# A two-pass attention kernel with a folded feed-forward layer: written step order and plain PSUM evacuation, against engine orders from a list scheduler, VectorE transposes and evacuation on three engines

## The chip, the cores and the metric

The kernel runs on one core of one Trainium2 chip. All times are device microseconds (us) of that core. A run's time is some 2 us longer than the span that the profile shows, because the span goes from the first to the last recorded instruction. Executions differ by a few tenths of a per cent; those whose clock state made them more than 1.5% slower than the fastest of the same kernel are called slow and are left out of every comparison here.

Engine names: PE is the matmul engine (PEld its weight loads), DVE is VectorE, ACT is ScalarE, POOL is GpSimd, SP is SyncE. In both kernels all loads of `x` are issued by GpSimd and are converted from float32 to fp16 on the way; all stores are issued by SyncE. "The queue" below is short for the 16 DMA engines that carry all transfers. PSUM is the memory into which the matmuls write; to evacuate a result is to copy it from there to SBUF, where the other tiles lie. The granted clock is the share of its full clock that PE was granted, by the profile.

## The reference, cut to what matters

```python
# x: (4, 12480, 128), inducing: (32, 128), w_in: (128, 2048), w_out: (2048, 128)
def mab(q, kv):
    s = (1/sqrt(128)) * (q @ kv.T)
    a = softmax(s)                     # + 1e-9 in the denominator
    return a @ kv
h   = mab(inducing, x)                 # per batch: 32 x 128, needs ALL of the batch's x
y   = mab(x, h)                        # per token: softmax over the 32 rows of h
out = gelu_exact(y @ w_in) @ w_out     # per token
```

The kernel uses that `y` is a mixture of 32 rows of `h` and that the argument of the GELU is small here: it puts the 32 rows of `h` through a quadratic form of the feed-forward layer once per batch (a chain of small steps ending in a 32 x 128 matrix `q`), and each token's output is its 32 softmax weights times `q`. Checks on the device add up whether that was admissible; if not, a general path runs.

What matters for time is the dependence. A batch's whole input (six tiles of 2048 tokens and a short tail) must be in before its `q` exists, and no output of that batch can be stored before that. So 27.7 MB come in, the two weights included (13.8 MB as fp16), and 25.6 MB go out, through the same 16 DMA engines, and output starts a batch later than input.

## The kernel before

One unit is 2048 tokens. The A side of a unit loads it, transposes it, makes scores against `inducing`, takes exp, turns the exponentials and gathers `hun += e1.T @ x`. The B side makes scores against `h`, takes exp, and writes four blocks of 512 columns of `o`, then stores them. The steps that the change touches:

```python
    def a_weights(bt, u):                      # turn the exponentials: PE, then a copy by VectorE
        e1 = bt.live.pop(("e1", u.idx))
        e1t_ps = ps.tile([128, 8, 128], FP16, tag="big", bufs=4)
        for ci in range(u.nci):
            nc.tensor.transpose(e1t_ps[: u.p, ci, : u.rows],
                e1[: u.rows, ci * u.p : (ci + 1) * u.p], identity_h[: u.rows, : u.rows])
        e1t = sb.tile([128, 4, 128], FP16, tag="e1t", bufs=2)
        nc.vector.tensor_copy(out=e1t[...], in_=e1t_ps[...])
    ...
    def b_out(bt, u, ci, on_act):              # one of four blocks of o
        at = ps.tile([128, 4, 128], FP32, tag="big", bufs=4)
        nc.tensor.matmul(at[...], e2[...], bt.q[...], start=True, stop=True)
        if on_act:   # four ScalarE quarters, each with its own scale
            ...
        else:
            nc.vector.tensor_tensor(out=ov[: u.p, ci, :, :], in0=at[...], in1=rr2[...], op=ALU.mult)
        if ci == u.nci - 1:
            nc.sync.dma_start(out=out[...], in_=o[...])
    ...
    LAG = n_u + 5                              # the B side runs 12 steps behind the A side
    def at_step(s):
        ...                                    # a0, a1, a2: units s, s-1, s-2; b0, b1: units s-12, s-13
        if a0: load_next(); a_transpose(bat(a0), a0, 0)
        if a1: a_score(bat(a1), a1)
        pump()                                 # one stage of the chain of a finished batch
        if b1: b_sum(...); b_out(..., 0, False); b_out(..., 1, lone)
        ...
    for _ in range(3): load_next()             # five tiles, then the weights, then three more tiles
    nc.gpsimd.dma_start(out=w_in_h, in_=moe_w_in)
    nc.gpsimd.dma_start(out=w_out_h, in_=...)
    for _ in range(3): load_next()
    for s in range(n_all + LAG + 1): at_step(s)
```

The framework's own scheduler may reorder what is written, within each engine, before it is compiled.

Of the kernel before, what the change touches and what calls it, by code (L numbers as in the profile page):

```python
# [8 lines left out]
FP32 = mybir.dt.float32  # L9
# [15 lines left out]

EPS = 2.0**-10
# [10 lines left out]
TP = TAIL // 2  # L37


class Unit:  # L40


    def __init__(self, b, idx):
        self.b = b
        self.idx = idx
        self.tail = idx == NFULL
        self.t0 = idx * SGT
        self.p = TP if self.tail else 128
        self.nj = 1 if self.tail else 4
        self.nci = 2 if self.tail else 4  # L50
        self.nc = self.nj * self.nci
        self.cols = self.nci * self.p
        self.rows = 32 * self.nj


@with_exitstack
def kernel(
# [22 lines left out]
    def a_load(u):  # L80
        xh = sb.tile([128, 16, 128], FP16, tag="xh", bufs=9)
        src = x[u.b, u.t0 : u.t0 + u.nc * u.p, :].rearrange("(p c) d -> p c d", p=u.p)
        nc.gpsimd.dma_start(out=xh[: u.p, : u.nc, :], in_=src)  # L83
        x_tiles[(u.b, u.idx)] = xh

    a_load(units[0][0])
# [9 lines left out]
    indT_ps = ps.tile([C, M], FP32, tag="misc")  # L96
# [30 lines left out]
    class Batch:  # L127
        def __init__(self, b):
            self.b = b
            self.rr2 = pre.tile([128, n_u, 4, 4], FP32, tag="rr2")  # L130
            nc.gpsimd.memset(self.rr2[:, NFULL, :, :], 1.0 / M)
            self.xT = xt_pool.tile([128, N], FP16, tag="xT", name=f"xT{b}")
            self.r1 = pre.tile([128, NFULL + 1], FP32, tag="r1")
            nc.gpsimd.memset(self.r1, 0.0)
# [6 lines left out]
    def a_transpose(bt, u, half):  # L141
        xh = x_tiles[(u.b, u.idx)]
        c0, c1 = (0, min(8, u.nc)) if half == 0 else (8, u.nc)
        if c1 <= c0:
            return
        tr = ps.tile([128, 8, 128], FP16, tag="big", bufs=4)
        for c in range(c0, c1):
            nc.tensor.transpose(  # L148
                tr[:, c - c0, : u.p], xh[: u.p, c, :], identity_h[: u.p, : u.p]
            )  # L150
        dst = bt.xT_of(u, c0, c1).rearrange("q (c p) -> q c p", p=u.p)
        if half == 0:
            nc.vector.tensor_copy(out=dst, in_=tr[:, : c1 - c0, : u.p])  # L153
        else:
            nc.scalar.activation(out=dst, in_=tr[:, : c1 - c0, : u.p], func=AF.Copy)  # L155

    def a_score(bt, u):
        s1 = ps.tile([128, 512], FP32, tag="sc", bufs=2)
        for j in range(u.nj):
            nc.tensor.matmul(  # L160
                s1[32 * j : 32 * j + 32, : u.cols],
                indT,
                bt.xT_of(u, j * u.nci, (j + 1) * u.nci),
# [3 lines left out]
        e1 = sb.tile([128, 512], FP16, tag="e1", bufs=2)  # L167
        nc.scalar.activation(
            out=e1[: u.rows, : u.cols],
            in_=s1[: u.rows, : u.cols],  # L170
            func=AF.Exp,
            scale=SCALE,
            accum_out=bt.r1[: u.rows, u.idx : u.idx + 1],
# [3 lines left out]
    def a_weights(bt, u):  # L177
        e1 = bt.live.pop(("e1", u.idx))
        e1t_ps = ps.tile([128, 8, 128], FP16, tag="big", bufs=4)
        for ci in range(u.nci):  # L180
            nc.tensor.transpose(  # L181
                e1t_ps[: u.p, ci, : u.rows],
                e1[: u.rows, ci * u.p : (ci + 1) * u.p],
                identity_h[: u.rows, : u.rows],
            )
        e1t = sb.tile([128, 4, 128], FP16, tag="e1t", bufs=2)
        nc.vector.tensor_copy(  # L187
            out=e1t[: u.p, : u.nci, : u.rows], in_=e1t_ps[: u.p, : u.nci, : u.rows]
        )
        bt.live[("e1t", u.idx)] = e1t  # L190

    def a_gather(bt, u):
        e1t = bt.live.pop(("e1t", u.idx))
        xh = x_tiles.pop((u.b, u.idx))
        for ci in range(u.nci):
            for j in range(u.nj):
                nc.tensor.matmul(  # L197
                    bt.hun[32 * j : 32 * j + 32, :],
                    e1t[: u.p, ci, 32 * j : 32 * j + 32],
                    xh[: u.p, j * u.nci + ci, :],  # L200
                    start=(u.idx == 0 and ci == 0),
                    stop=(u.tail or (u.idx == NFULL - 1 and j > 0)) and ci == u.nci - 1,
                )
# [15 lines left out]
    def check_gelu(bt, pt, hs):  # L219


        b = bt.b
        zsq = pre.tile([128, NBLK, M], FP32, tag="zsq")
        nc.scalar.activation(out=zsq, in_=pt, func=AF.Square)
        ssq = pre.tile([128, NBLK], FP32, tag="ssq")
        nc.vector.tensor_reduce(out=ssq, in_=zsq, axis=AX.X, op=ALU.add)
        left = pre.tile([128, NBLK], FP32, tag="left")
        nc.vector.scalar_tensor_tensor(
            out=left, in0=hs, scalar=-1.0 / M, in1=hs, op0=ALU.mult, op1=ALU.mult
        )  # L230
        nc.vector.tensor_tensor(out=left, in0=left, in1=ssq, op=ALU.add)
        quart = pre.tile([128, NBLK], FP32, tag="quart")
        nc.vector.scalar_tensor_tensor(
            out=quart, in0=ssq, scalar=1.0 / 6.0, in1=ssq, op0=ALU.mult, op1=ALU.mult
        )
        nc.vector.tensor_tensor(out=left, in0=left, in1=quart, op=ALU.add)
        sums = pre.tile([128, 2], FP32, tag="sums")
        nc.vector.scalar_tensor_tensor(
            out=quart,
            in0=left,  # L240
            scalar=(2.0 * CGELU / EPS) ** 2 * M,
            in1=left,
            op0=ALU.mult,
            op1=ALU.mult,
            accum_out=sums[:, 0:1],
        )
        nc.vector.tensor_reduce(out=sums[:, 1:2], in_=ssq, axis=AX.X, op=ALU.add)
        tot_ps = ps.tile([128, 2], FP32, tag="misc")
        nc.tensor.matmul(tot_ps, ones_f, sums, start=True, stop=True)
        right = pre.tile([128, 2], FP32, tag="right")  # L250
        nc.vector.tensor_copy(out=right, in_=tot_ps)
        nc.vector.tensor_tensor(
            out=checks[:, b, 4:5], in0=right[:, 0:1], in1=right[:, 1:2], op=ALU.is_le
        )
        nc.vector.tensor_scalar(
            out=checks[:, b, 5:6],
            in0=right[:, 1:2],
            scalar1=Z_LOW * DFF * M,
            scalar2=None,
            op0=ALU.is_ge,  # L260
        )

    def precompute(bt):
        hun_sb = pre.tile([128, C], FP32, tag="hun_sb")
        nc.scalar.activation(out=hun_sb, in_=bt.hun, func=AF.Copy)
        r1c = pre.tile([128, 1], FP32, tag="r1c")
        nc.vector.tensor_reduce(out=r1c, in_=bt.r1, axis=AX.X, op=ALU.add)
        r1s = pre.tile([128, M], FP32, tag="r1s")
        nc.vector.tensor_scalar(
            out=r1s, in0=stack4, scalar1=r1c, scalar2=None, op0=ALU.mult  # L270
        )
        yield
        h_ps = ps.tile([128, 2, M], FP32, tag="misc")
        nc.tensor.matmul(h_ps[:, 0, :], ones_f, r1s, start=True, stop=True)
        nc.tensor.matmul(h_ps[:, 1, :], hun_sb, stack4, start=True, stop=True)
        yield
        rr1 = pre.tile([128, M], FP32, tag="rr1")
        nc.vector.reciprocal(out=rr1, in_=h_ps[:, 0, :])
        in_range(rr1, 1.0 / R_HIGH, 1.0 / R1_LOW, bt.b, 0)
        bt.hT = pre.tile([128, M], FP16, tag="hT")  # L280
        nc.vector.tensor_tensor(out=bt.hT, in0=h_ps[:, 1, :], in1=rr1, op=ALU.mult)

        yield
        pt_ps = ps.tile([128, NBLK, M], FP32, tag="misc")
        for blk in range(NBLK):
            nc.tensor.matmul(
                pt_ps[:, blk, :],
                w_in_h[:, blk * 128 : (blk + 1) * 128],
                bt.hT,
# [3 lines left out]
        yield  # L293
        pt = pre.tile([128, NBLK, M], FP32, tag="pt")
        nc.scalar.activation(out=pt, in_=pt_ps, func=AF.Copy)
        hs = pre.tile([128, NBLK], FP32, tag="hs")
        nc.vector.tensor_reduce(out=hs, in_=pt, axis=AX.X, op=ALU.add)
        slope = pre.tile([128, NBLK], FP32, tag="slope")
        nc.vector.tensor_scalar(
            out=slope,  # L300
            in0=hs,
            scalar1=2.0 * CGELU / M,
            scalar2=0.5,
            op0=ALU.mult,
            op1=ALU.add,
        )
        offs = pre.tile([128, NBLK], FP32, tag="offs")
        nc.vector.scalar_tensor_tensor(
            out=offs,
            in0=hs,  # L310
            scalar=CGELU / (M * M),
            in1=hs,
            op0=ALU.mult,
            op1=ALU.mult,
        )
        sl = pre.tile([128, NBLK, M], FP32, tag="sl")
        nc.vector.tensor_tensor(
            out=sl,
            in0=pt,
            in1=slope.unsqueeze(2).broadcast_to([128, NBLK, M]),  # L320
            op=ALU.mult,
        )
        gl = pre.tile([128, NBLK, M], FP16, tag="gl")
        nc.vector.tensor_tensor(
            out=gl,
            in0=sl,
# [66 lines left out]
    def b_out(bt, u, ci, on_act):  # L393
        if ci >= u.nci:
            return
# [310 lines left out]
```

## Time and profile before

| kernel before | |
|---|---|
| time, median of 3 | 160.44 us (160.09 to 160.69) |
| span of the profiled run | 158.4 us, mean granted clock 0.923 |
| busy: PE, DVE, ACT, POOL | 122.8, 106.0, 77.2, 17.9 us |
| DMA queues' packet time | 45.7% + 39.8% + 0.7% of the span: 136.5 us |
| first and last store issued | 49.8 and 147.3 us |
| transfers of the last store all but over | 152.3 us (last packet ends at 152.6) |

Here are lines of the profile page of the kernel before. In the lines of digits, each digit is one of 40 slices of the span (3.96 us each) and gives the busy share in tenths; DMA is the mean of the 16 DMA engines, and GB/s is what they moved in each slice. The last line is from the table of DMA issues: the count, the size of each, and the median time from issue to landing.

```profile
span 158.4 us, 3683 instructions
...
DVE  2122321547967997977988988788869979799100
...
DMA  2999999999999999999999766243469865899930
GB/s 43 207 211 214 197 202 218 213 213 211 214 212 213 301 305 321 313 318 316 267 312 354 304 267 265 103 166 132 161 286 408 366 269 211 346 387 408 430 137 14
...
out_dram<-o SPq DMA_DIRECT2D x24, 1024.0 KB, 4.4
```

The DMA digits are 9 from the second slice to slice 22, that is to about 87 us. There the loads end: the last is issued at 79.4 us and lands 7.2 us later, at 86.6. The digits then fall to 7, 6, 6, 2, 4, 3, 4, 6: the queue has little to do, although about 18 of the 25.6 MB of output still have to leave. In the median a store lands 4.4 us after its issue, of which the transfer alone takes 2.4; so most stores of this kernel do not queue, they are waited for.

The next lines are the view of busy time in chosen windows, for the kernel before. Columns: start and end, length; busy us and number of instructions of PE, PEld, DVE, ACT and POOL; then the granted clock, the DMA share (it adds up the times of packets, and reads somewhat above 1 where the queue is full) and GB/s.

```profile
core 0: us, PE busy (x) PEld busy (x) DVE busy (x) ACT busy (x) POOL busy (x), PEclk, DMA share, GB/s
3.00:92.00 89.00, 77.50 (x1026) 47.36 (x1027) 58.16 (x157) 44.74 (x87) 15.88 (x36) 0.98 1.06 255
92.00:152.30 60.30, 45.28 (x437) 20.56 (x434) 47.43 (x141) 31.13 (x83) 0.11 (x1) 0.88 0.69 280
```

Up to 92 us the transfers hardly pause (only from 88 us on does the share fall, to 0.68). After 92 us there are 60.3 us at share 0.69, which is 41.6 us of transfer and 18.7 us of idle queue, while VectorE still has 47.4 us of work and PE 45.3 us. The largest single term of the time that could be saved stands here.

### The profile page before, as it was taken

The page shows a single profiled execution, that of the slowest core. Times are in us where ns is not written, and L with a number is a line of the kernel's source. Part 1 is how long each engine was busy: PE and PEld are TensorE (multiplying, and loading weights), DVE is VectorE, ACT ScalarE, POOL GpSimd, SP SyncE. Part 2 cuts the span into 40 slices and gives each one's busy share as a digit, 9 for nine tenths or more (in the row PEclk, how much of TensorE's full clock was granted, in tenths as well). Part 3 has the DMA queues.
Part 4 walks back from the last instruction along what each step waited for, and adds up shares of the span by engine and source line. Part 5 has one row for each costly group of instructions (what it writes and reads, how often), then busy time and mean ns, then how long its engine had stood idle before and what let it go on. Part 6 is the DMA issues. An engine that isn't in the chain of part 4 may idle for free. (4 is left out here: it accounts for less than half of the span.)

```text
span 158.4 us, 3683 instructions
## 1 busy us (share of the span) xinstructions
PE 122.8 (78%) x1459; PEld 67.9 (43%) x1459; DVE 106.0 (67%) x303; ACT 77.2 (49%) x171; POOL 17.9 (11%) x44
## 2 busy tenths in 40 slices
PE   0388957899999999988899999878998578984000
PEld 0356634676655555454444645435344233321000
DVE  2122321547967997977988988788869979799100
ACT  3035642578574555734445548344476824885000
POOL 7811120222111201110110000000000000000000
PEclk9999996999999999999999999999999955699655
DMA  2999999999999999999999766243469865899930
GB/s 43 207 211 214 197 202 218 213 213 211 214 212 213 301 305 321 313 318 316 267 312 354 304 267 265 103 166 132 161 286 408 366 269 211 346 387 408 430 137 14
DMA packets 10091, 39.73 MB, mean 251 GB/s; under 512 B 2992, under 2 KB 3792, under 8 KB 6992
## 3 DMA queue, kind: packets, MB, share of 16 engines
q0 software_dynamic: 6112, 13.83, 45.7%
q1 hardware_dynamic: 3952, 25.58, 39.8%
q8 instruction: 13, 0.21, 0.5%
q14 instruction: 14, 0.11, 0.2%
HBM read 27.67 MB, written 25.56 MB: 336 GB/s over the span
## 5 line engine op out<-in xcount | busy, mean ns | idle before, releaser
L148 PE MATMUL tr<-identity_h,xh 128*128 128x128 f16 x392 | 35.2, 237 | 7.3 <-DMA xh<-in_x_dram 6.2
L148 PEld LDWEIGHTS <-xh 128*128 128x128 f16 x392 | 26.2, 107 | 16.5 <-issue 7.7
L83 POOL DMA_DIRECT2D xh<-in_x_dram x28 | 15.1, 538 | 59.6 <-PE hun_888 L197 17.2
L187 DVE COPY e1t<-e1t_ps 128x512 f16<-128x512 f16 (+1 forms) x28 | 10.8, 387 | 11.9 <-PE e1t_ps L181 11.5
L417 DVE TENSOR_TENSOR o<-at,rr_426 128x512 f32<-128x512 f32 (+1 forms) x26 | 16.1, 652 | 1.0 <-PE at L401 0.8
L417 DVE TENSOR_TENSOR o<-at,rr_118 128x512 f32<-128x512 f32 (+1 forms) x26 | 16.1, 652 | 0.9 <-PE at L401 0.7
L417 DVE TENSOR_TENSOR o<-at,rr_883 128x512 f32<-128x512 f32 (+1 forms) x20 | 12.8, 658 | 0.2
L153 DVE COPY xT_120<-tr 128x1024 f16<-128x1024 f16 (+1 forms) x7 | 4.4, 630 | 10.8 <-PE tr L148 10.8
L417 DVE TENSOR_TENSOR o<-at,rr_1484 128x512 f32<-128x512 f32 (+1 forms) x19 | 11.4, 659 | 0.1
L155 ACT ACTIVATE xT_120<-tr 128x1024 f16<-128x1024 f16 x6 | 6.1, 1021 | 10.4 <-PE tr L148 10.4
L197 PEld LDWEIGHTS <-e1t 128*32 128x32 f16 x392 | 8.1, 97 | 5.8 <-issue 3.2
L360 PEld LDWEIGHTS <-hT 128*32 128x32 f16 x100 | 4.4, 94 | 10.3 <-issue 9.8
L160 PEld LDWEIGHTS <-indT 128*32 128x32 f16 x100 | 4.9, 94 | 8.9 <-issue 6.8
L155 ACT ACTIVATE xT_1486<-tr 128x1024 f16<-128x1024 f16 x6 | 6.1, 1022 | 4.9 <-PE tr L148 4.7
L410 ACT ACTIVATE o<-at,rr_1484 128x128 f32<-128x128 f32 (+1 forms) x25 | 7.2, 369 | 2.3 <-PE at L401 1.6
L155 ACT ACTIVATE xT_885<-tr 128x1024 f16<-128x1024 f16 x6 | 6.1, 1022 | 4.4 <-PE tr L148 4.2
L410 ACT ACTIVATE o<-at,rr_883 128x128 f32<-128x128 f32 (+1 forms) x21 | 6.1, 373 | 2.9 <-DVE rr_883 L387 2.8
L155 ACT ACTIVATE xT_428<-tr 128x1024 f16<-128x1024 f16 x6 | 6.1, 1019 | 1.4 <-PE tr L148 1.3
L153 DVE COPY xT_428<-tr 128x1024 f16<-128x1024 f16 (+1 forms) x7 | 4.4, 627 | 2.0 <-PE tr L148 1.9
L348 DVE TENSOR_TENSOR q<-q_ps,strand 128x512 f16<-128x512 f32 x4 | 2.8, 692 | 3.8 <-PE q_ps L346 3.8
L153 DVE COPY xT_1486<-tr 128x1024 f16<-128x1024 f16 (+1 forms) x7 | 4.3, 621 | 0.8 <-PE tr L148 0.8
L153 DVE COPY xT_885<-tr 128x1024 f16<-128x1024 f16 (+1 forms) x7 | 4.3, 620 | 0.6 <-PE tr L148 0.6
(434 smaller groups left out, 231.1 us busy)
## 6 DMA issues: line engine op xcount, KB each, us to landing
out_dram<-o SPq DMA_DIRECT2D x24, 1024.0 KB, 4.4
xh<-in_x_dram POOLq DMA_DIRECT2D x24, 512.0 KB, 11.5
w_in_h<-in_moe_w_in_dram POOLq DMA_DIRECT2D x1, 512.0 KB, 14.4
w_out_h<-in_moe_w_out_dram POOLq DMA_DIRECT2D x1, 512.0 KB, 17.3
out_dram<-o SPq DMA_DIRECT2D x4, 96.0 KB, 4.9
xh<-in_x_dram POOLq DMA_DIRECT2D x4, 48.0 KB, 10.8
ind_s<-in_inducing_dram SPq DMA_DIRECT2D x1, 16.0 KB, 1.8
```

The lines of the kernel that those rows point to most:

```text
L83: nc.gpsimd.dma_start(out=xh[: u.p, : u.nc, :], in_=src)
L148: nc.tensor.transpose(tr[:, c - c0, : u.p], xh[: u.p, c, :], identity_h[: u.p, : u.p])
L153: nc.vector.tensor_copy(out=dst, in_=tr[:, : c1 - c0, : u.p])
L155: nc.scalar.activation(out=dst, in_=tr[:, : c1 - c0, : u.p], func=AF.Copy)
L160: nc.tensor.matmul(s1[32 * j : 32 * j + 32, : u.cols], indT, bt.xT_of(u, j * u.nci, (j + 1) * u.nci), start=True, stop=True,)
L187: nc.vector.tensor_copy(out=e1t[: u.p, : u.nci, : u.rows], in_=e1t_ps[: u.p, : u.nci, : u.rows])
L197: nc.tensor.matmul(bt.hun[32 * j : 32 * j + 32, :], e1t[: u.p, ci, 32 * j : 32 * j + 32], xh[: u.p, j * u.nci + ci, :], start=(u.idx == 0 ...
L348: nc.vector.tensor_tensor(out=bt.q, in0=q_ps.unsqueeze(1).broadcast_to([128, 4, 128]), in1=strand.unsqueeze(2).broadcast_to([128, 4, 128]) ...
L360: nc.tensor.matmul(s2[32 * j : 32 * j + 32, : u.cols], bt.hT, bt.xT_of(u, j * u.nci, (j + 1) * u.nci), start=True, stop=True,)
L410: nc.scalar.activation(out=ov[: u.p, ci, j, :], in_=at[: u.p, j, :], func=AF.Copy, scale=rr2[: u.p, ci, j : j + 1],)
L417: nc.vector.tensor_tensor(out=ov[: u.p, ci, :, :], in0=at[: u.p, : u.nj, :], in1=rr2[: u.p, ci, : u.nj].unsqueeze(2).broadcast_to([u.p, u. ...
```

## The change

The intent: make every engine's instruction order from a plan rather than by hand; start output as soon as the first batch allows; and spread the work that VectorE does over ScalarE and GpSimd, so that transfers never wait. The diff, cut to its core:

```diff
+class Plan:                       # a list scheduler: pieces with cost per engine, dependencies, buffers
+    def run(self):
+        ...                       # repeatedly takes the piece that could start first; ties within 0.12 us
+                                  # go by key, and a batch's chain (key -1) may win by up to 0.4 us
+        self.pieces.sort(key=lambda p: p.at)
+        for p in self.pieces: p.emit(p.engine)
+def pin_order(tc):                # ties each instruction to the one before it on its engine, so
+    ...                           # that the framework's scheduler can't reorder them

-    xh ... bufs=9                 +    xh ... bufs=XBUFS        # 11
-    for _ in range(3): load_next()          # weights behind five tiles
+    for k, u in enumerate(order):
+        add_load(u)
+        if k == NFULL: add_weights()        # weights behind all seven tiles of batch 0
+    for i in range(FILLERS): ...            # 8 matmuls on zeros before the first tile arrives

-            nc.tensor.transpose(e1t_ps[...], e1[...], identity_h[...])
-        nc.vector.tensor_copy(out=e1t[...], in_=e1t_ps[...])
+        # a_score now puts tokens on partitions in blocks of 32; e1 is held as fp16 pairs
+        nc.vector.transpose(out=pairs(e1t)[: u.p, :n], in_=pairs(e1)[: u.p, :n])   # 32x32 blocks, as int32

-    b_out: block 1 on ScalarE in the last steps only, all others on VectorE
+    AWAY = (0,)                   # block 0: plain copy by ScalarE, then scaled in place by GpSimd
+    other blocks: VectorE (0.61 us) or four ScalarE quarters (1.0 us), as the plan decides
-    LAG = n_u + 5
+    key (k + BEHIND, n)           # B side of unit k ranks with A side of unit k + 13, where both could start
```

Smaller parts: three PSUM buffers for scores and small results instead of two and one, three buffers `e2` instead of two, the square of the check on VectorE instead of ScalarE, and the general path's loop over batches rolled into a loop on the device.

## The prediction

> **What bounds the kernel before** (busy time in chosen windows). (a) 3 to 50 us: only loads move, 207 to 214 GB/s, DMA share above 1; first store issued at 49.8 us. (b) 50 to 92 us: DMA share 1.00 at 307 GB/s, PE 92%, DVE 85% busy. (c) 92 to 147 us: loads are over, DMA at 0.44, 0.58, 0.78; DVE is 81 to 89% busy and ends the chain of waits. Then 4.6 us until the last store lands (152) and 6.4 us of closing (span 158.4).
>
> DMA work: 24.4 loads of 0.52 MB at 212 GB/s, 2.47 us each, 60 us; two weights 5 us; 24.4 stores of 1.05 MB at 430 GB/s, 2.44 us each, 59.5 us: 125 us. From 3 to 152 us that leaves 24 us of idle DMA, nearly all in (c): stores begin too late, then compute cannot feed them.
>
> **What the change does.**
> - Weights behind batch 0's tiles: batch 0 complete about 5 us earlier (the transposes waited 3 us for a tile at 22 to 25 us). PE fillers spare some half-clock transposes (eight: 1.03 against 0.62 us), worth little while DMA-bound.
> - The chain goes first and output follows at once, instead of a fixed lag of 12 steps: first store at about 34 us (batch 0 landed 21, gathered 24, chain 8, first tile 2) instead of 49.8.
> - VectorE, counted in the instruction order: evacuations with scaling 85 to 52 (0.60 us start to start), xT copies 24 to 30, PSUM copies of e1t (0.34 us) replaced by transposes of 256 words, which I estimate at 0.34 us too (the pace of the measured copies; Trainium skill, "VectorE: DVE Perf Modes", the three transpose paths: 311 ns for a 128x128 in bf16; no trace yet). About 101 to 87 us.
> - ScalarE: 44 to 80 scaled quarters (0.26 us), 24 plain copies (0.51), 6 fewer xT copies (0.92): about 69 to 84 us.
> - GpSimd: 24 multiplications of 128x512. Skill, "GPSIMD Engine Reference", 4497 ns for 2048 columns: my estimate 1.1 to 1.3 us each, 29 us, beside 15 us of DMA issue; off the critical path, for a block of o has 2.4 us.
> - PE: 104 transposes gone (0.32 us per unit); pieces stay whole, where single score matmuls between `at` matmuls cost 0.32 us each, as much as four together. About 115 to 95-100 us.
>
> **Sum.** DMA (125 us) then exceeds every engine: DVE 87, ACT 84, PE about 98. If it never idled: 3 + 125 + 1 + 6.4 gives a span of 136, time 138 us. I allow 5 us of idle DMA, as the pinned order follows a model whose errors turn into waits, and PE at 80% in the mixed stage is close. Prediction 143 us, 11% faster; range 138.5 to 149. Faster 0.95, same 0.04, slower 0.01.
>
> **What would show it.** First store issued at 31 to 37 us; DMA at 300 or more GB/s from there to the end, no stretch of 4 us under 0.5; DVE busy 85 to 95 us; transposes 0.35 to 0.45 us each; GpSimd multiplications 1.1 to 1.4 us; last compute at about 131.
>
> **What would make it wrong.** GpSimd stuck in order: a load waiting for a free buffer holds back a multiplication, hence a store, or the reverse. Multiplications far slower beside VectorE. The granted clock at half in the store-only end (0.63 at 130 to 140), which makes `at` 0.60 instead of 0.38 us. Loads and stores together slower than apart. Strided weights (e1t in pairs) or score inputs slowing PE.

## More of the kernel before

The stores, from the timeline of SyncE in the kernel before (start, length up to the last, then the group):

```profile
49.79 97.89 SPq L425 DMA_DIRECT2D out_dram<-o  x28
```

The first of 28 stores is issued at 49.79 us, and the group ends 97.89 us later.

## The result, and the profile after

Ratios are the mean time of one kernel's fast runs over the mean of the other's in the same rounds, with a 95% interval, so they are not quite the ratio of the medians that are quoted.

| | before | after |
|---|---|---|
| time, median (rounds of this comparison) | 160.56 us | 141.1 us (140.5 to 141.8) |
| ratio | | 0.8796 (0.8751 to 0.8841) |
| span, clock of the profiled run | 158.4, 0.923 | 138.7, 0.918 |
| busy PE, DVE | 122.8, 106.0 | 101.6, 96.4 |
| busy ACT, POOL | 77.2, 17.9 | 88.5, 42.6 |
| DMA packet time (share times span) | 136.5 us | 98.6%: 136.8 us |
| first store issued, transfers of the last all but over | 49.8, 152.3 | 43.2, 134.2 (last packet ends at 134.7) |

The change is 12.0% faster. The packet time is the same: the same transfers are packed into 20 us less. The same lines of the page, for the kernel after (a slice is 3.47 us):

```profile
span 138.7 us, 3625 instructions
...
DVE  1354334264999997996989998756999879888000
...
DMA  3999999999999999999999999999889799999960
GB/s 30 197 213 214 215 208 188 216 214 211 214 213 211 267 314 318 307 336 340 325 315 277 295 314 312 318 345 413 369 361 378 309 418 380 390 425 418 416 236 7
...
out_dram<-o SPq DMA_DIRECT2D x24, 1024.0 KB, 8.3
```

The DMA digits are 9 almost throughout; the lowest before the end is a 7. The time from issue to landing of a store has gone from 4.4 to 8.3 us: stores now stand in a queue. The windows of the kernel after, with the columns as before:

```profile
3.00:92.00 89.00, 72.99 (x1126) 44.95 (x1126) 65.96 (x187) 61.33 (x145) 28.29 (x41) 0.96 1.07 262
92.00:134.20 42.20, 28.57 (x245) 12.14 (x245) 30.16 (x97) 27.16 (x81) 12.47 (x12) 0.87 0.95 384
```

Compare with the two rows of before. Up to 92 us both kernels keep the queue full, and both have moved nearly the same: 89 us at 255 GB/s are 22.7 MB, at 262 GB/s 23.3 MB. So the earlier start of the stores has gained 0.6 MB by then, some 1.5 us at the rate of the end, and of that the kernel before lost 1.3 us by idling from 88 us on. What the earlier stores carried, the loads gave up: the last load of the kernel after lands at 97.6 us instead of 86.6. The difference is in what the engines had got done under the same transfers: VectorE 66.0 against 58.2 us, ScalarE 61.3 against 44.7, GpSimd 28.3 against 15.9. After 92 us the kernel after has 42.2 us at share 0.95: 40.1 us of transfer, 2.1 idle. Of the 19.7 us by which the span shrank, 16.6 are idle queue time taken away after 92 us (18.7 less 2.1), 1.5 are less transfer left at 92 us (41.6 less 40.1), and 1.6 are a shorter closing behind these windows (6.1 and 4.5 us to the end of the span).

The stores in the timeline of SyncE, kernel after:

```profile
43.19 85.96 SPq L648 DMA_DIRECT2D out_dram<-o  x28
```

The first is at 43.19 us, where the prediction had 31 to 37; the last is issued at about 128.

The chain of waits that ended last, first by engine and then by line, in the kernel after:

```profile
DVE 12%; DMA 10%; PE 9%; ACT 7%; issue 2%; POOL 1%; DVEq 0%; ACTq 0%; SPq 0%
DMA out_dram<-o 10%; DVE o L638 6%; PE at L601 4%; ACT o L631 3%; PE s L558 2%; ACT e L570 2%; ACT o L263 1%; DVE xT L261 1%; DVE left L502 1%; POOL o L623 1%; DVE zsq L490 1%; ACT e L298 1%; PE q_ps L450 1%; DVE hit L333 0%; ACT pt L388 0%
```

`DMA out_dram<-o` is now its first entry: blocks of `o` wait until an earlier store has left its buffer. In the kernel before, no DMA appears in that part of the page (shown here in the same form); the chain could be followed only for the last 3 us, and is VectorE writing `o`:

```profile
DVE 2%; PE 0%; issue 0%
DVE o L417 1%; DVE hit L209 0%; PE tot_ps L518 0%; DVE tot L526 0%; DVE failed L528 0%; DVE rr_1484 L387 0%
```

### The profile page after: what moved, and what is told of

It reads as the page before. It is cut to its first block, busy times and chain, and to the rows that moved or that the text cites. A ratio compares the mean times of both kernels' runs of the same rounds, so it can differ in the third digit from the quotient of the medians.

```text
span 138.7 us, 3625 instructions
## 1 busy us (share of the span) xinstructions
PE 101.6 (73%) x1371; PEld 57.1 (41%) x1371; DVE 96.4 (69%) x284; ACT 88.5 (64%) x226; POOL 42.6 (31%) x60
## 5 line engine op out<-in xcount | busy, mean ns | idle before, releaser
L601 PE MATMUL at<-q,e 128*128 128x512 f16 (+1 forms) x104 | 35.6, 387 | 5.9 <-ACT o L631 1.4
L623 POOL TENSOR_TENSOR o<-o,rr 128x512 f32<-128x512 f32 x24 | 25.0, 1042 | 43.5 <-ACT o L263 35.2
L638 DVE TENSOR_TENSOR o<-at,rr 128x512 f32<-128x512 f32 (+1 forms) x55 | 34.6, 659 | 5.3 <-DMA out_dram<-o 2.4
L272 PE MATMUL tr<-identity_h,xh 128*128 128x128 f16 x392 | 28.3, 223 | 5.3 <-DVE o L638 2.4
L261 DVE COPY xT<-tr 128x1024 f16<-128x1024 f16 (+1 forms) x32 | 20.4, 649 | 12.3 <-PE tr L272 12.1
L631 ACT ACTIVATE o<-at,rr 128x128 f32<-128x128 f32 (+1 forms) x85 | 24.2, 370 | 3.4 <-DMA out_dram<-o 2.5
L298 ACT ACTIVATE e<-s 128x512 f16<-128x512 f32 (+1 forms) x28 | 15.3, 546 | 11.5 <-PE s L286 10.9
L263 ACT ACTIVATE xT<-tr 128x1024 f16<-128x1024 f16 (+1 forms) x20 | 19.1, 960 | 5.2 <-PE tr L272 5.2
L263 ACT ACTIVATE o<-at 128x512 f32<-128x512 f32 x24 | 14.5, 603 | 5.5 <-DMA out_dram<-o 3.4
L570 ACT ACTIVATE e<-s 128x512 f16<-128x512 f32 (+1 forms) x28 | 14.8, 559 | 3.9 <-PE s L558 3.9
L320 PE MATMUL hun<-xh,e1t 128*32 128x128 f16 x392 | 11.0, 230 | 6.1 <-DVE e1t L312 6.1
L601 PEld LDWEIGHTS <-e 128*128 128x128 f16 (+1 forms) x104 | 9.1, 102 | 12.6 <-issue 8.0
L582 PEld LDWEIGHTS <-e 128*128 128x128 f16 (+1 forms) x104 | 5.6, 99 | 5.7 <-ACT e L570 2.4
## 6 DMA issues: line engine op xcount, KB each, us to landing
xh<-in_x_dram POOLq DMA_DIRECT2D x24, 512.0 KB, 18.7
w_out_h<-in_moe_w_out_dram POOLq DMA_DIRECT2D x1, 512.0 KB, 18.7
```

Source lines behind the costliest of these rows:

```text
L261: nc.vector.tensor_copy(out=out, in_=in_)
L263: nc.scalar.activation(out=out, in_=in_, func=AF.Copy)
L272: nc.tensor.transpose(tr[:, c - c0, : u.p], xh[: u.p, c, :], identity_h[: u.p, : u.p])
L298: nc.scalar.activation(out=e1[: u.p, : u.nc // 2, :, :], in_=s1[: u.p, : u.nc, :].rearrange("r (a b) i -> r a i b", b=2), func=AF.Exp, sca ...
L320: nc.tensor.matmul(bt.hun[32 * j : 32 * j + 32, :], e1t[: u.p, c // 2, :, c % 2], xh[: u.p, c, :], start=u.idx == 0 and c < 4, stop=c + 4 ...
L570: nc.scalar.activation(out=e2[: u.rows, : u.cols], in_=s2[: u.rows, : u.cols], func=AF.Exp, scale=SCALE,)
```

## The experiments

The theory after the result: the kernel after is set by the DMA queue, and the gain is the idle queue time after 92 us, filled because the planned order brings more of the engines' work in front of 92 us. The rivals: (1) the gain comes from less work on the engines, that is from VectorE's transposes and from the blocks given to ScalarE and GpSimd; (2) it comes from the first batch being complete earlier; (3) GpSimd, which issues loads and scales blocks in one order, now holds something back. The twelve runs were made in three groups, each on one chip beside its own runs of the kernel before (medians 160.94, 160.69 and 160.09).

### Halving the stores, in both kernels

To see what binds each kernel, half of the bytes of each store were left out, with all the computing kept. The results are wrong (half of the output is never written).

```diff
-  out=out[base : base + u.nc * u.p, :].rearrange("(p c) d -> p c d", p=u.p),
-  in_=o[: u.p, : u.nc, :],
+  out=out[base : base + u.nc * u.p, :].rearrange("(p c) d -> p c d", p=u.p)[:, : u.nc // 2, :],
+  in_=o[: u.p, : u.nc // 2, :],
```

For the kernel after:

> The changed kernel, but each store moves only half of its columns (wrong result on purpose); the order of instructions is the same. Theory D (the changed kernel waits on the DMA queues from 3 us to 134 us): 24.4 stores cost 1.2 us less each, 30 us of DMA work go, and the time falls to where compute binds, 115 to 128 us. Rival C (the pinned order and the engines set the pace, the queues are merely kept full by it): within 2% of 141, 138 or more.

For the kernel before:

> The kernel before with stores of half the columns (wrong on purpose). Theory D says of it that only 50 to 92 us was bound by DMA and that VectorE and PE set the rest, so little is won: 150 to 160 us. Rival R (the kernel before was bound by DMA all along, as its 125 us of transfers suggest, and the change only shortens the ends): 130 to 142.

Measured: the kernel after fell to 130.6 us (0.8167 of before, 0.8092 to 0.8242; span 128.7). The kernel before only fell to 157.45 us (0.9816, 0.9736 to 0.9897; span 154.6), though the same 30 us of packet time or so were taken from it. The fall of the kernel after is clear, but it stops 2.6 us above the range that the theory had given (115 to 128): the engines bind earlier than expected. The windows of the halved kernels, the kernel after first, from 75 us to its last store:

```profile
75.00:123.00 48.00, 39.43 (x461) 19.37 (x457) 43.34 (x125) 39.55 (x114) 16.62 (x16) 1.00 0.56 208
```

The halved kernel before, from 75 us to its last store:

```profile
75.00:149.00 74.00, 60.98 (x644) 29.96 (x643) 62.60 (x181) 39.83 (x100) 1.27 (x4) 0.93 0.42 149
```

In the halved kernel after, VectorE is busy 43.3 of 48 us, and the queue has a share of 0.56. So the queue does bind the kernel after, but the next limit, the engines, lies only 10 us below: a saving of transfers beyond that would give nothing more. In the kernel before, halving the stores leaves the queue at 0.42 and the time nearly unchanged: that kernel was bound by its engines in their order, and a saving of transfers would have helped it little.

### The order alone

The kernel after with everything but the order put back: transposes of `e1` on PE with VectorE's copy, no blocks for GpSimd, no fillers, nine tiles, weights behind five tiles. The plan (made anew for these pieces), the pinning and the small changes to buffers stay.

```diff
-XBUFS = 11            +XBUFS = 9
-AWAY = (0,)           +AWAY = ()
-FILLERS = 8           +FILLERS = 0
-        if k == NFULL: add_weights()
+        if k == 4: add_weights()
-  a_turn: nc.vector.transpose(...)       # and the score layout that goes with it
+  a_flip: nc.tensor.transpose(...) x4;  a_turn: nc.vector.tensor_copy(...)
```

> The changed kernel with its parts undone and only the planned, pinned order and the merged pieces kept: e1t by PE and PSUM copy, no ScalarE copy plus GpSimd multiplication, weights after five tiles, no fillers, 9 buffers of x; planned anew. Theory O (the order alone keeps the queues full, and the parts only make slack behind them): 141 to 146. Rival P (each part is covered by the slack of the others, together they carry the gain): 149 or more.

Measured: 144.69 us, 0.9025 (0.8943 to 0.9106): 9.7 of the 12 per cent. Its windows:

```profile
3.00:92.00 89.00, 74.50 (x1098) 50.38 (x1098) 64.30 (x184) 50.50 (x139) 15.41 (x29) 0.92 1.07 262
92.00:138.50 46.50, 33.74 (x369) 16.05 (x361) 40.32 (x117) 33.25 (x103) 0.00 (x0) 0.97 0.86 349
```

Up to 92 us it moves just as much as the kernel after, at 262 GB/s. Then 46.5 us at 0.86, against 60.3 at 0.69 in the kernel before. VectorE has been given no relief at all here (104.9 us in total against 106.0), and yet it had 64.3 us of it behind it at 92 us instead of 58.2, and fewer pauses afterwards (40.3 busy of 46.5 us). Its stores start only 1.4 us earlier than in the kernel before (49.79), so an earlier first store is not what the order gains by:

```profile
48.40 86.39 SPq L657 DMA_DIRECT2D out_dram<-o  x28
```

This run leaves two things open. The general path rolled into a loop is still in it: from the last packet of a store to the end of the span it takes 3.5 us, the kernel before 5.8, so some 2.3 of the 15.7 us by which its span is shorter are probably not the order's. And the plan also chooses the engine of many copies and blocks (ScalarE is busy 83.8 us here, 77.2 before); that choice, the cheaper matmuls described next and the order of the pieces as such were not taken apart.

The order also makes the same matmuls cheaper. Both kernels run 1459 of them, at nearly the same clock (0.923 and 0.928), and PE was busy 122.8 us before and 108.2 here. By line: the 392 gather matmuls took 16.1 us before and 11.1 here, the score matmuls of the B side 14.9 and 9.3. Four 32-column matmuls written next to each other run together in parts of the array; the framework's order had put others between them (a gather of 16 came out as 1, 13 and 2). The Trainium skill, "TensorE: Matmul & The Clock Gate", Part 3 (packing small matmuls), describes multiple matmuls running concurrently in one array when each has its own tile of it. The two totals agree with that.

### The order without the pin

```diff
-    pin_order(tc)
```

> The changed kernel, all parts kept, but the planned order is not pinned, so the framework's own scheduler may reorder, and the instruction lists do differ on every engine. Theory O: matmul groups are split again and output blocks fall behind, idle DMA returns after 95 us: 146 to 156. Rival P: the work saved is what counts, and the half-store run shows 10 us of slack: under 144.

Measured: 149.76 us, 0.9321 (0.9247 to 0.9394). The windows of this run:

```profile
3.00:92.00 89.00, 71.41 (x979) 43.84 (x979) 52.59 (x152) 51.50 (x124) 25.99 (x39) 0.83 1.06 256
92.00:145.00 53.00, 41.76 (x393) 18.30 (x392) 39.23 (x118) 35.68 (x103) 14.66 (x15) 0.81 0.77 314
```

Here the framework may still reorder what the plan wrote, and about 5 points of the 12 are lost (0.9321 against 0.8796, in two groups of runs). Up to 92 us it has done only 52.6 us of VectorE work; after that the queue has 0.77. The profiled run had a lower clock (0.817), but that isn't the main cause: another run of it with a clock of 0.885 took 149.39 us, where the kernel after with the same clock took 141.98 us (in another group). Of its gain over the kernel before, some 4 us are closing (1.8 us from the last packet to the end of the span, 5.8 before). The converse, the kernel before with its written order pinned, does not build: the framework reports a deadlock, so it could not be tried. What pinning alone does to the written order stays open.

### The loading side: weights behind the first batch, fillers, eleven tiles

The order alone, with these three put in again:

```diff
 # against the order alone
-XBUFS = 9             +XBUFS = 11
-FILLERS = 0           +FILLERS = 8
-        if k == 4: add_weights()
+        if k == NFULL: add_weights()
```

> Planned and pinned order, weights behind batch 0, fillers and 11 buffers of x, but e1t by PE and no ScalarE copy plus GpSimd multiplication. Theory L (of the 3.6 us that the parts add to the order, most comes from the loading side): 141 to 143. Rival S (the savings of VectorE and PE matter only when both are gone, each alone was covered by the other): 143.5 to 145, like the order alone.

Measured, in five rounds: 141.26 us, 0.8832 (0.8799 to 0.8865). With the kernel after in the same group:

> The changed kernel once more, as the control on this chip for the three runs beside it: 0.88 of before, about 141 us. Both theories alike.

That measured 140.28 us, 0.8784 (0.8733 to 0.8835). The intervals overlap. So the order and the loading side give all but about half a point; what VectorE's transposes and the two extra engines add is under what these rounds resolve. Between the order alone and this kernel lie 1.9 points, though across two groups of runs; the three parts of the loading side were not taken apart.

Late weights alone, in the kernel before:

```diff
-    for _ in range(3): load_next()     +    for _ in range(5): load_next()
     ... weights ...
-    for _ in range(3): load_next()     +    for _ in range(1): load_next()
```

> The kernel before, with the two weights loaded behind batch 0's tiles and nothing else. Both theories: the PE's 3 us wait at 22 to 25 us goes, and the engines, which bind from there on, shift by about that: 157 to 159. If the start does not reach the end (the stages after it have slack): 160 to 161.

Measured: 159.65 us, 0.9948 (0.9867 to 1.0028): no difference that these runs resolve, and a median between the two ranges that were expected. A first batch that is complete earlier brought nothing measurable to this kernel, whose B side starts at a fixed step. Rival (2) falls as a cause by itself; within the planned order it has at most a share of the 1.9 points of the loading side.

### The VectorE transposes: taken out of the kernel after, put into the kernel before

```diff
 # a_peturn, against the kernel after
-  a_turn: nc.vector.transpose(...)
+  a_flip: nc.tensor.transpose(...) x4;  a_turn: nc.vector.tensor_copy(...)
```

> The changed kernel with the weights e1t turned by PE and copied out of PSUM as before, planned anew. Theory D: PE gets 24 x 0.32 us back, VectorE about the same; PE was 84 to 91% busy in 50 to 90 us, and PSUM buffers are shared, 0 to 4 us slower, 141 to 145. Rival V (the VectorE transposes are the gain): 148 or more.

Measured: 141.23 us, 0.8803 (0.8738 to 0.8868), against 0.8796 for the kernel after: no difference.

```diff
 # b_turn: the kernel before, with a_score, a_exp, a_turn, a_gather of the kernel after
-            a_weights(bat(a1), a1)
+            a_turn(bat(a1), a1)
```

> The kernel before with only the VectorE transposes of e1t (and the score layout they need). PE loses 24 x 0.32 us, VectorE stays. Theory O: the order around it still splits groups and leaves the output late: 155 to 160. Rival P (PE work is what binds the kernel before): all of 8 us, 151 to 154.

Measured: 165.51 us, 1.0278 (1.0178 to 1.0379). Both expectations missed: it is slower, with 96 fewer matmuls. Since the interval reaches under 1.02, it isn't certain that the loss exceeds two per cent. Three views of the trace of this run say where a part of it comes from. First, the timeline of GpSimd, whose sequencer issues the loads; in brackets is the idle time before and what ended it:

```profile
11.68 0.53 POOL L83 DMA_DIRECT2D xh<-in_x_dram  x1 [1.88 <-DMA xh<-in_x_dram]
...
31.70 2.11 POOL L83 DMA_DIRECT2D xh<-in_x_dram  x4 [19.25 <-PE hun L195]
```

No load of `x` is issued for 19.25 us, until a tile comes free, and it comes free by the gather `hun`. The timeline of PE in the same stretch:

```profile
24.77 2.05 PE L148 MATMUL tr<-identity_h,xh 128*128 128x128 f16 x18 [6.80 <-DMA xh<-in_x_dram]
...
30.84 0.76 PE L195 MATMUL hun<-xh,e1t 128*32 128x128 f16 x32
```

PE has waited 6.80 us for a tile at 24.77 us and does the first gather at 30.84 only. The gather needs the exponentials, and the timeline of ScalarE has the first exp here:

```profile
27.62 0.59 ACT L173 ACTIVATE e<-s 128x512 f16<-128x512 f32 x1
```

Its scores were done at 12.84 us, but it stands behind ScalarE's copies of the first six tiles. So the framework's scheduler, given the new pieces, put work on later tiles ahead of the exp and of the gather that would have freed a buffer, and the queue ran dry: its share from 20 to 34 us was 0.81, where the kernel before has 1.15 and the kernel after 1.22. (The granted clock was lower too, 0.87 to 0.88 in the fast runs against 0.91 to 0.93 before; how much of the loss that makes was not separated.) The same transposes in a pinned order cost nothing. Rival (1) falls as far as transposes go: alone they lose, and within the planned order they gain nothing measurable.

### No blocks for GpSimd

```diff
-AWAY = (0,)
+AWAY = ()
```

> The changed kernel without ScalarE copy plus GpSimd multiplication: those 24 blocks go to VectorE or ScalarE, in an order planned anew. Theory D: engines have slack beside the queues before 95 us, but not in 100 to 128 us (DVE 97% in 100 to 110), so 0 to 3 us slower, 141 to 144. Rival V (moving the evacuations off VectorE is what made the gain): 24 x 0.6 us return, 148 or more.

Measured: 142.15 us, 0.8861 (0.8783 to 0.8939), against 0.8796 (0.8751 to 0.8841) for the kernel after. The ratio is 0.7% higher and the intervals overlap. Twenty-four multiplications on a third engine are worth one microsecond or nothing. With the queue as the limit that is what the theory asks for.

### Two attempts to beat both kernels

The queue is idle in the first 3 us and less than full in a few places behind 92 us. The first attempt loads `w_in` as float32 through SyncE's queue at the very start, and lets VectorE or ScalarE convert it, so that GpSimd's queue has one transfer less:

```diff
+    w_in_f = consts.tile([128, DFF], FP32)
+    nc.sync.dma_start(out=w_in_f, in_=moe_w_in)
-        for dst, src in ((w_in_h, moe_w_in), (w_out_h, w_out_view)):
+        for dst, src in ((w_out_h, w_out_view),):
+            plan.add(key(15), {"DVE": 1.3, "ACT": 1.9}, lambda e: evacuate(e, w_in_h, w_in_f), kept)   # unit 1
```

> The changed kernel with the first weight loaded by SyncE's queue as f32 from 1.2 us on and cast by VectorE, in the time when the queues stand idle (before 3 us; 16 to 30 GB/s in 0 to 3 us of the trace). Theory D (time = work of the queues, started earlier): 0.8 to 1.5 us faster than the control, 0.990 to 0.995 of it. Rival E (the end is set by engines between 100 and 118 us, where the queues idle 2 us): no change or slower.

Measured: 143.27 us, 0.8919 (0.8867 to 0.8972), against 0.8784 for the kernel after in the same group: a miss. Windows of this kernel:

```profile
2.00:5.00 3.00, 1.86 (x5) 0.76 (x6) 1.50 (x18) 0.00 (x0) 2.92 (x7) 1.00 0.86 287
5.00:20.00 15.00, 10.39 (x129) 6.87 (x128) 5.67 (x12) 6.41 (x10) 4.78 (x8) 0.77 1.07 220
98.00:114.00 16.00, 13.57 (x127) 5.75 (x127) 14.29 (x48) 11.71 (x38) 4.80 (x5) 0.79 0.75 307
```

The same windows of the kernel after, run in the same group:

```profile
2.00:5.00 3.00, 1.86 (x5) 0.76 (x6) 1.51 (x18) 0.00 (x0) 2.92 (x7) 1.00 0.79 115
5.00:20.00 15.00, 10.70 (x176) 7.04 (x175) 5.50 (x13) 8.82 (x15) 4.53 (x8) 1.00 1.07 212
98.00:114.00 16.00, 13.75 (x162) 6.21 (x150) 15.12 (x48) 14.21 (x45) 6.06 (x6) 0.99 0.90 368
```

The aim was reached, 287 instead of 115 GB/s from 2 to 5 us. But the first tile of `x` then shared the queue and landed later (its transposes start at 8.79 us instead of 6.48), PE did 129 instead of 176 matmuls from 5 to 20 us at a lower clock (0.77 instead of 1.00), and the plan, which was made anew, came out with a share of 0.75 instead of 0.90 from 98 to 114 us. Work put into the queue early doesn't make the kernel shorter if it delays the batch that everything waits for. How much of the loss is that delay, how much the other plan and how much the lower clock (0.83 to 0.88 in its fast runs, 0.89 to 0.92 in the kernel after) was not separated. The second attempt adds a second block for GpSimd:

```diff
 # against c_wsp
-AWAY = (0,)           +AWAY = (0, 2)
```

> The same, and a second block of each unit goes to ScalarE copy (0.5 us instead of 1.04) and GpSimd. ScalarE and VectorE were 83 to 97% busy in 100 to 118 us, where the queues idled about 2 us. Theory D: those gaps close, a further 0.5 to 1.5 us, 138 to 139.5 in all. Rival G: GpSimd becomes late with its multiplications (1.04 us each, two a unit, beside 0.55 us of a load), stores wait for it, and it gets slower than c_wsp.

Measured: 144.25 us, 0.9024 (0.8988 to 0.9059), about one per cent slower again, as its rival G expected. GpSimd was busy 68.4 us, and SyncE's stores waited for a block from it 16 times, 19.3 us in all, against 3 times and 4.7 us in the kernel after. So rival (3) is real with two blocks, and small with one. No version that beats the kernel after was found.

## Why the prediction was right

Predicted were 143 us, with a range of 138.5 to 149; measured were 141.1. The main mechanism, that the change lets the transfers run almost without a pause and that they then set the time, was right, and halving the stores showed it. Point by point:

- **"DMA (125 us) then exceeds every engine."** Right, with the term a little too small: counting the 89 us up to 92 us as full, and 40.1 us after, the transfers take 129 us. The margin was smaller than the sum suggests: the engines in their order need a span of 128.7 us with halved stores, 10 us less than they have. The busy times alone (PE 101.6, VectorE 96.4) would have promised a margin twice as large or more.
- **"I allow 5 us of idle DMA."** It was about 2 us. **"6.4 us of closing"** became 4.5, probably since the general path is rolled into a loop: the four traces of kernels without that loop end 5.7 to 5.8 us after the last packet of a store, the ten with it 1.8 to 4.8. The prediction had not priced that, and no run tested it alone. So four errors, 4 us too little and 3, 2 and 1 us (its allowance for the last landing) too much, nearly cancelled: 3 + 129 + 2 + 4.5 is 138.5, the measured span is 138.7. That the number came within 2 us is partly luck.
- **"Stores begin too late" and "first store at about 34 us".** This step failed, in its size and in its worth. The first store came at 43.2 us. Batch 0 was gathered at 25.0, one microsecond late; the chain took 9.8 us instead of 8 (PE's clock was 0.76 from 20 to 34 us, and its matmuls with `w_out` stood behind other planned work); and from `q` (34.7) to the first store it took 8.5 us instead of 2, because the plan ranks batch 1's A side ahead of batch 0's B side. And it didn't matter: while loads fill the queue, an earlier store only displaces a load (the last load landed at 97.6 us instead of 86.6). Up to 92 us both kernels moved nearly the same bytes, with first stores 6.6 us apart.
- **"Then compute cannot feed them."** Right, and this is where the gain lies: 18.7 us of idle queue after 92 us became 2.1. The prediction's sign for it, no 4 us under a share of 0.5, held: the lowest of eight such windows from 80 to 112 us had 0.79. Its other sign, 300 GB/s or more from the first store on, was missed in three slices (267, 277 and 295).
- **The costs.** The transposes took 0.40 us on average and the full ones 0.43 (0.35 to 0.45 predicted; the skill's "VectorE: DVE Perf Modes", the three transpose paths, has 311 ns for a smaller one). GpSimd's multiplications took 1.04 us, just under the 1.1 to 1.4 predicted (an estimate from the 4497 ns for 2048 columns in the skill's "GPSIMD Engine Reference", 3.1, a quarter of which is 1.12). VectorE was busy 96.4 us where 85 to 95 were predicted: the counts were multiplied by 0.60 us from start to start, while records of busy time have 0.66 for the same evacuation, 3 us over 55 of them, and some small operations were stretched (see the last section). PE had 101.6 (95 to 100), ScalarE 88.5 (84).

These are the groups of the kernel after (line, engine, operation, tiles, count; busy us, mean ns; idle before and its cause):

```profile
L638 DVE TENSOR_TENSOR o<-at,rr 128x512 f32<-128x512 f32 (+1 forms) x55 | 34.6, 659 | 5.3 <-DMA out_dram<-o 2.4 <-PE s L558 0.8 <-PE at L601 0.6
...
L623 POOL TENSOR_TENSOR o<-o,rr 128x512 f32<-128x512 f32 x24 | 25.0, 1042 | 43.5 <-ACT o L263 35.2 <-DVE rr L593 6.2 <-DVE xT L261 2.0
...
L312 DVE STREAM_TRANSPOSE e1t<-e 128x256 int32<-128x256 int32 (+1 forms) x28 | 11.0, 398 | 0.2 <-ACT e L298 0.2
```

For comparison, the copy of the kernel before that the transposes replaced:

```profile
L187 DVE COPY e1t<-e1t_ps 128x512 f16<-128x512 f16 (+1 forms) x28 | 10.8, 387 | 11.9 <-PE e1t_ps L181 11.5
```

The copy took 387 ns and the transposes 398 (the full ones 420 and 434): on VectorE this exchange is neutral, and only PE was relieved. And in the kernel after, the evacuation's first cause of idle time is `DMA out_dram<-o`, a full store queue.

What the prediction didn't see is which part of the change does the work. It listed savings on every engine as if each contributed. The runs put nearly 10 of 12 per cent on the order (some 1.4 of these probably on the shorter closing that came with it), most of the rest on the loading side, and nothing resolved on transposes and evacuation. The planned order cannot be separated further from the pinning: the plan without the pin gives 6.8%, and the pin without the plan could not be run.

## What to carry to other kernels

Where a profile shows a full queue first and idle queue time later, ask what the engines could have done during the full stretch: moving their work ahead of the point where loads end was worth more here than an earlier first store, which only took the place of a load. The Trainium skill, "Perfetto Trace Analysis", Optimization Strategy, says of kernels with several regimes that "performance may be improved by interleaving those regimes", and the order alone, 9.7% faster here with its closing, is an instance. An order that was worked out must also be kept through the compiler (6.8% without the pin, 12% with it), and an operation that is cheaper by itself can lose in an order that wasn't made for it (VectorE's transposes: 2.8% slower in the old order, nothing in the new one).

## What the Trainium skill lacked or had wrong

- "SBUF — State Buffer", "SBUF: two separate sides": the page says that a VectorE instruction with two SBUF inputs and a GpSimd instruction that reads SBUF exclude each other for the whole instruction. The runs agree, and add a size for a small operation. Timeline of the kernel after:

```profile
38.46 0.17 DVE L502 TENSOR_TENSOR left<-left,ssq 128x16 f32<-128x16 f32 x1
38.55 1.31 DVE L504 SCALAR_TENSOR_TENSOR quart<-ssq 128x16 f32<-128x16 f32 x1
...
38.77 1.05 POOL L623 TENSOR_TENSOR o<-o,rr 128x512 f32<-128x512 f32 x1
```

  The 128 x 16 operation of L504, whose two inputs lie in SBUF, took 1.31 us (the other three of it 0.16 to 0.17), ending just after GpSimd's multiplication did. By these records it had started 0.22 us before it, which does not fit the page's rule that the first to start keeps the ports; but starts on GpSimd are only roughly recorded, so this is left open. A second case fits the rule: L502 at 98.13 us took 0.92 us, while a multiplication of GpSimd ran from 97.98 to 99.02. In the run without blocks for GpSimd the mean of this operation is 168 ns, and in the kernel before it has this group line:

```profile
L233 DVE SCALAR_TENSOR_TENSOR quart<-ssq 128x16 f32<-128x16 f32 x4 | 0.7, 169 | 0.0
```

  Evacuations, which read one tensor from PSUM and only the scale from SBUF, did not change (full ones 679 to 682 ns before, 680 after).
- "DMA: Bandwidth & Descriptors", Specifications, gives about 358 GB/s as the limit of HBM for a core, beside a fabric ceiling of 435. In this program of one core the slices at the end, with stores alone, moved up to 425 GB/s, so the smaller figure did not bind; the page says so only further down, with its measured single-core rates, and its note on the three figures still has the HBM side bind transfers between HBM and SBUF, which these stores do not bear out.
- I found no time on that page for a load that converts from float32 to fp16. Here such loads ran at 207 to 214 GB/s of what they write, so 0.52 MB take 2.47 us, as long as a plain store of twice the bytes (2.44 us); counted by the 1.05 MB that it reads, such a load is as fast as the store.
- "VectorE: DVE Perf Modes", the three transpose paths, gives only 128 x 128 in bf16. Packed pairs of fp16 as 32-bit words, 128 x 256 words, took 398 ns on average over the 28 (four of them smaller), and the full ones 434, for twice the elements and four times the bytes.
- "TensorE: Matmul & The Clock Gate", Part 3, on packing, does not say what it costs when other matmuls get between those of a group, and "TensorEngine Tiling (Array Packing)", Key Properties, says that a change of tiling mode drains the engine, but gives no time: 392 gather matmuls took 16.1 us in the framework's order and 11.1 us kept together.
- No page that was read says how much the framework's own reordering matters: the same plan was 0.9321 of before without the pin and 0.8796 with it (in different groups of runs).
